# A hand-scheduled attention and routed-FFN kernel: GpSimd waits for VectorE behind each gather and scatter, and the schedule builder takes its settings from a table by chunk

## The chip, the cores and the metric

The kernel runs on one core of a Trainium2 chip. The metric is the device time of one launch in microseconds (us); lower is better. PE is TensorE, DVE is VectorE, ACT is ScalarE, POOL is GpSimd, and SP is the engine that issues most of the DMAs.

## What is computed

Eight batches, each with 3136 tokens of 256 features. First an attention without softmax, then a feed-forward step for the 128 best tokens of each batch:

```python
scores = (1 / S) * z @ z.T                     # z: 8 x 3136 x 64, symmetric scores
x = u * (np.maximum(scores, 0) ** 2 @ v)       # u, v: 8 x 3136 x 256
for b in range(8):
    s = x[b] @ w_gate
    top = the 128 tokens with the largest s
    h = np.maximum(x[b, top] @ w1, 0)          # w1: 256 x 1024
    out[b, top] = x[b, top] + sigmoid(s[top])[:, None] * (h @ w2)
```

## The kernel before

Each batch is cut into seven chunks of tokens (six of 512, one of 64), and each chunk into slots of pairs of key blocks. For a slot PE makes the scores (tile `sc`), ACT rectifies them into `a`, ACT or DVE squares `a`, and the square is split into two parts that PE can multiply at full rate: `hi` (a rounding, on ACT) and `lo` (the square less `hi`, a subtraction with two inputs in SBUF, on DVE or POOL). PE multiplies both parts with `V`, which is split in the same way, into the accumulator `acc`. The scores are symmetric, so DVE also transposes each square (`aT`), SP stores it to DRAM (`squares`), and later slots read it back (`qk`) in place of computing it; these are split too. At a chunk's end `acc` becomes `sum`, is multiplied with `u` (`ut`), transposed (`x`) and stored to `out`. PE works in halves of 64 rows, two at a time.

The routing of a batch runs beside the attention of the next ones. DVE counts against thresholds until the 128 tokens are found and forms their numbers (`ids`). POOL then gathers the rows from `out` with an indirect DMA (`xe<-out,ids`), PE runs the two layers, and POOL scatters the result back with another indirect DMA (`out<-y,ids`). There are 8 gathers, 8 scatters and one small first gather (`junk<-in_v`).

The order of all instructions on each engine is fixed when the kernel is built. A list scheduler keeps a model of the engines (class `Clock`) and a list of jobs for ACT, DVE, POOL and SP. `job` puts a job in, `begins_at` says when it could begin, `advance` emits the earliest one, and the loop at the end picks the next work for PE (`choices`, `emit`). Some constants set how eager it is: `NEAR` (how far ahead of PE the others are filled), `SPARE` (an extra cost of DVE when a `lo` may go to POOL or DVE), `EARLY` (how long an operand must have been ready before PE prefers it), `FAR` and a literal 2.0 (how long a step of the routing waits behind its operand), and `QUIET`. The model knows that an operation of POOL right behind an indirect DMA can hold up a DVE operation that is under way (`at_once` and `hold` in `note`). In the trace nearly every instruction carries the same helper's line (L265), so it is read by tile names.

Of the kernel before, what the change touches and what calls it, by code (L numbers as in the profile page):

```python
# [29 lines left out]
EARLY = 0.4  # L30
# [3 lines left out]
SPARE = 0.6  # L34
MARGIN = 0.3
QUIET = 9
SOON = -0.2
FAR = 4.0
SLACK = 2.0
WARM = 6.6  # L40
# [50 lines left out]
class Clock:  # L91
# [3 lines left out]
    def __init__(self):  # L95
        self.at = {"pe": 0.9, "act": 1.15, "dve": 0.85, "pool": 0.5, "sp": 0.75}
        self.queue = self.mark = 0.0
        self.writes, self.reads, self.before, self.rings = {}, {}, {}, {}
        self.port = {"dve": (0.0, 0.0), "pool": (0.0, 0.0)}
        self.newest, self.alone = {}, {"dve": 0.0, "pool": 0.0}  # L100
        self.kept = self.since = -1.0
        self.planned = self.known = False
        self.half, self.by_half, self.long = [0.0, 0.0], False, False
# [91 lines left out]
    def note(self, by, op, outs, ins):  # L195
# [171 lines left out]
def attention_then_routed_ffn(ctx: ExitStack, tc: tile.TileContext, zt, ut, v, wg, w1, w2, cst, cst16, keys, outs, at, cap):  # L367
# [87 lines left out]
    NEAR = 0.3  # L455
# [7 lines left out]

    def begins_at(j, e):
        if j.ok and not j.ok():
            return None
        rings = j.rings() if callable(j.rings) else j.rings
        if not all(x.free() for x in rings):
            return None
        ready = j.ready() if callable(j.ready) else j.ready  # L470
        ready = max([ready] + [x.when() + 0.05 for x in rings])
        t = max(clock.at[e], ready)
        if len(j.on) > 1:

            def done(o):
                t = max(clock.at[o], ready)
                a, z = clock.port.get({"pool": "dve", "dve": "pool"}.get(o), (0.0, 0.0)) if j.locks else (0.0, 0.0)
                return max(t + j.took[o], z + j.took[o] - 0.14 if a <= t < z else 0.0)

            if any(done(o) < done(e) for o in j.on if o != e):  # L480
                return None
        return t

    def advance(upto):

        while True:
            best = None
            for e, jobs in pending.items():
                if clock.at[e] >= upto + NEAR:
                    continue  # L490
                for j in jobs:
                    t = begins_at(j, e)
                    if t is None or t >= upto + NEAR:
# [12 lines left out]
    def quiet():  # L506

        k = now[0]
        if k >= kmax:
            return True  # L510
        b, c = slots[k][:2]
        n = len(todo.get(k, ()))
        return c == WHOLE or not (k == ends[b, c] and n <= QUIET or k == begins[b, c] and n >= 11 and c > 0)
# [63 lines left out]
    def takes(n):  # L577
        return {"pool": 0.15 + 0.00219 * n, "dve": 0.16 + 0.00104 * n + SPARE, "act": 0.19 + 0.00083 * n}

# [9 lines left out]
    def load_consts():  # L589
# [16 lines left out]
        nc.sync.dma_start(st[:, : cst16.shape[1]], cst16)  # L606
        zero_ids = moe.tile([P, 1], I32, name="zero_ids", tag="ids", bufs=3)
        nc.vector.memset(zero_ids, 0)
        job("pool", now[0], lambda e: first_gather(zero_ids), [zero_ids])
        job("pool", now[0] + 2, lambda e: use_consts(c_sb, st), lambda: max(clock.after(x) for x in (st, c_sb)) + SLACK)  # L610
        consts["run"] = w_run
# [13 lines left out]
    def more_consts():  # L625

        def place():
            consts["place"] = const.tile([P, 1], F32, name="place")
            nc.vector.tensor_reduce(consts["place"], consts["before"], axis=AX.X, op=ALU.add)
            consts["wg_col"] = const.tile([P, NK], F32, name="w_col")  # L630
            consts["wg_row"] = const.tile([P, NK, P], F32, name="w_row")

        def clear():
# [4 lines left out]
        def column(h):  # L638
            w_row, w_col = consts["wg_row"][:, h], consts["wg_col"][:, h : h + 1]
            nc.vector.scalar_tensor_tensor(  # L640
                w_row[:, :Q], consts["run"][:, h * Q : (h + 1) * Q], 1.0, consts["fold"][:, :Q],
                op0=ALU.mult, op1=ALU.mult, accum_out=w_col,
            )

        def row(h):
            nc.vector.tensor_scalar(consts["wg_row"][:, h], consts["ones"], consts["wg_col"][:, h : h + 1], None, op0=ALU.mult)

        ready = lambda: "ident" in consts and quiet()
        return [("dve", fn, (), (), ready) for fn in (place, clear, *[lambda f=f, h=h: f(h) for h in range(NK) for f in (column, row)])]
# [419 lines left out]
    def half_scores(k):  # L1069
# [27 lines left out]
        def high(e):  # L1097
            hi = hi_ring.take("hi", F32R)
            set_part(k, hi, None)
            for to in (hi[:REST, 0], hi[low_part, 1]):  # L1100
                nc.scalar.activation(to, st["a"], AF.Square, scale=1 / SCALE)
            took = {"dve": 0.16 + 0.00104 * CH + SPARE, "act": 0.3 + 0.00083 * CH}
            job("dve|act", k, square, [st["a"], st["s"], hi[:REST, 0], hi[low_part, 1]], took=took)
# [38 lines left out]
    def scores(k):  # L1142
# [22 lines left out]
        def rise(e):  # L1165
# [6 lines left out]
            else:  # L1172
                job("act", k, high, lambda: max(clock.after(st["a"]), room_when(k)) + 0.05, ok=lambda: room_for(k))
# [260 lines left out]
    def finish(b, c, h):  # L1434
# [10 lines left out]
        def total(e):  # L1445
# [4 lines left out]
            if merged(b) and c == FIFTH:  # L1450
                took["dve"] -= SPARE
# [510 lines left out]
    def route_both(couple, i):  # L1962
# [96 lines left out]
        def choose_both():  # L2059
# [9 lines left out]
            inside = st["ps"][:, 3 * P :]  # L2069
# [45 lines left out]
    def choose(st, r0):  # L2115
# [11 lines left out]
        inside = st["ps"][:, 3 * P :]  # L2127
# [219 lines left out]
    def scatter_of(couple, i):  # L2347
        b, st = couple["of"][i], couple["st"][i]
        nc.gpsimd.indirect_dma_start(outs[b], bass.IndirectOffsetOnAxis(ap=st["ids"], axis=0), couple["y"][:, i], None)

# [103 lines left out]
    def expert(b, st, n):  # L2454
# [21 lines left out]
        def gather():  # L2476
# [7 lines left out]
            )  # L2484
            st["xe"] = xe
# [176 lines left out]
        def scatter():  # L2662
            nc.gpsimd.indirect_dma_start(
                outs[b], bass.IndirectOffsetOnAxis(ap=st["ids"][:m, :], axis=0), st["y"][:m], None
            )

# [134 lines left out]
    at_slot(first_of[0, 3], lambda: chain_of(more_consts(), 5))  # L2801
# [43 lines left out]
    def step_when(x):  # L2845
# [6 lines left out]
        late = 0.1 if x.lag == 20 else 0.05 if x.lag in (-9, -20) else SOON if "gathered" in end else MARGIN if x.lag < 0 or closing else 2.0 if x.lag == 1 else FAR  # L2852
        return max([x.ready + late] + [clock.after(y) + late for y in reads] + [r.when() + 0.05 for r in rings])

    def choices():
# [12 lines left out]
        for n, (i, k, x) in enumerate(near_):  # L2868
# [6 lines left out]
            if t <= clock.at["pe"] + 0.02 - EARLY:  # L2875
                return got
# [62 lines left out]
    def begin_slot():  # L2939
        for fn in plan.pop(now[0], ()):  # L2940
# [11 lines left out]
    while now[0] < kmax or any(x.steps for x in chains) or any(pending.values()):  # L2952
# [4 lines left out]
        sure = [x for x in got if x[0] <= t + 0.02 - EARLY]  # L2957
# [47 lines left out]
```

## Time and profile before

| | |
|---|---|
| median of 3 runs | 2019.31 us (2017.54 to 2019.4) |
| the profiled execution's own time | 2021.63 us |
| its span, first to last instruction | 2019.9 us |
| PE busy | 1989.0 us, 98% of the span |
| DVE, ACT, POOL busy | 77%, 73%, 77% |
| mean granted clock of PE | 0.997 |

PE is busy nearly all the time. Busy time alone hides one thing: a matmul that runs at the lower of PE's two clock levels (1.2 instead of 2.4 GHz) is also busy, for longer.

### The profile page before, as it was taken

Reading aid. Unit: us, or ns where it says so; the run is one execution under the profiler, and the core shown is the slowest. Engines: PE = TensorE matmul, PEld = TensorE weight load, DVE = VectorE, ACT = ScalarE, POOL = GpSimd, SP = SyncE. Lnnn points to the kernel's source line nnn. Section 1 sums busy time; section 2 is a strip of 40 time slices with the busy share of each in tenths; the row PEclk is TensorE's granted clock in tenths of the full one; section 3 lists DMA queues with packets and bytes.
Section 4 is the critical chain, followed back from the end, with each engine's and each line's share of the span. In section 5 each row is a group of like instructions: output and inputs, shape, how many; then the busy total and the mean of one; then the engine's idle time right before and its main releaser. Section 6 shows DMA issues by size and latency. Waiting matters only on the chain. (4 is left out here: it accounts for less than half of the span.)

```text
span 2019.9 us, 45873 instructions
## 1 busy us (share of the span) xinstructions
PE 1989.0 (98%) x17311; PEld 1651.1 (82%) x17311; DVE 1553.6 (77%) x2585; ACT 1482.5 (73%) x1835; POOL 1558.8 (77%) x1095
## 2 busy tenths in 40 slices
PE   9999999999999999999999999999999999999998
PEld 6788878888788888788878889887788888878776
DVE  7776787667988767767798866797679676897886
ACT  8876688777877669776887657876578876877652
POOL 8798887779878677878888767796687777887762
PEclk9999999999999999999999999999999999999999
DMA  6989867876787867878767786777866868767862
GB/s 193 258 237 247 208 190 220 213 190 168 206 235 207 207 173 218 241 181 194 193 202 214 211 218 188 208 216 204 217 173 198 235 177 202 191 181 199 218 160 95
DMA packets 421615, 408.50 MB, mean 202 GB/s; under 512 B 128910, under 2 KB 329232, under 8 KB 421392
## 3 DMA queue, kind: packets, MB, share of 16 engines
q1 hardware_dynamic: 420224, 403.07, 74.3%
q8 instruction: 135, 2.21, 0.5%
q0 software_dynamic: 800, 2.10, 0.3%
q14 instruction: 88, 0.72, 0.1%
q10 hardware_dynamic: 368, 0.39, 0.1%
HBM read 230.08 MB, written 175.37 MB: 201 GB/s over the span
## 5 line engine op out<-in xcount | busy, mean ns | idle before, releaser
L265 PE MATMUL acc<-hi,V 64*128 64x512 f32 x8832 | 1176.7, 390 | 8.6 <-DVE sum L265 4.6
L265 PEld LDWEIGHTS acc<-hi,V 64*128 64x128 f32 x8832 | 865.9, 185 | 162.6 <-DVE sum L265 9.0
L265 PE MATMUL acc<-lo,V 64*128 64x512 f32 x4272 | 632.5, 390 | 2.5 <-POOL lo L265 1.6
L265 POOL TENSOR_TENSOR lo<-a,hi 128x512 fp32r<-128x512 f32 x308 | 467.6, 1528 | 175.4 <-ACT a L265 84.4
L265 POOL TENSOR_TENSOR lo<-qk,hi 128x512 fp32r<-128x512 f32 x313 | 481.5, 1553 | 83.5 <-ACT hi L265 58.6
L265 PEld LDWEIGHTS acc<-lo,V 64*128 64x128 f32 x4272 | 423.0, 185 | 82.8 <-POOL lo L265 8.5
L265 ACT ACTIVATE hi<-a 128x1024 fp32r<-128x1024 f32 (+2 forms) x390 | 353.6, 907 | 108.6 <-PE acc L265 85.6
L265 DVE STREAM_TRANSPOSE aT<-a 128x512 f32<-128x512 f32 (+2 forms) x622 | 383.5, 646 | 42.5 <-ACT a L265 30.4
L265 ACT ACTIVATE a<-a 128x1024 f32<-128x1024 f32 (+1 forms) x349 | 330.7, 949 | 79.1 <-DVE a L265 69.0
L265 DVE TENSOR_TENSOR lo<-a,hi 128x512 fp32r<-128x512 f32 x236 | 269.4, 1146 | 138.3 <-ACT a L265 61.1
L265 ACT ACTIVATE a<-sc 128x1024 f32<-128x1024 f32 (+2 forms) x344 | 324.8, 945 | 65.8 <-PE sc L265 35.7
L265 ACT CAST hi<-qk 128x1024 fp32r<-128x1024 f32 x240 | 249.8, 1047 | 127.7 <-PE acc L265 71.2
L265 DVE TENSOR_TENSOR lo<-qk,hi 128x512 fp32r<-128x512 f32 x167 | 176.5, 1068 | 51.4 <-ACT hi L265 45.1
L265 PE MATMUL sc<-ZH 64*128 64x512 f32 (+2 forms) x728 | 157.8, 380 | 5.8 <-DVE a L265 3.0
L265 PE MATMUL sc<-ZL,ZH 64*128 64x512 f32 (+2 forms) x728 | 156.4, 376 | 0.1
L265 POOL TENSOR_TENSOR lo<-own,hi 128x256 fp32r<-128x256 f32 x87 | 92.4, 1081 | 72.6 <-ACT hi L265 42.7
L265 POOL TENSOR_TENSOR ut<-x,w_run 128x512 f32<-128x512 f32 x90 | 135.8, 1520 | 11.8 <-DVE x L265 10.8
L265 PE MATMUL sc<-ZH,ZL 64*128 64x512 f32 (+2 forms) x680 | 136.3, 370 | 0.0
L265 PE MATMUL acc<-lent,V 64*128 64x512 f32 x1008 | 130.2, 390 | 2.9 <-DVE sum L265 1.4
L265 POOL TENSOR_TENSOR ut<-sum,ut 128x512 f32<-128x512 f32 x70 | 97.6, 1395 | 26.9 <-DVE sum L265 23.8
L265 PEld LDWEIGHTS acc<-lent,V 64*128 64x128 f32 x1008 | 97.7, 184 | 23.7 <-DVE sum L265 3.1
L265 DVE SCALAR_TENSOR_TENSOR a<-a 128x512 f32<-128x512 f32 (+2 forms) x85 | 100.2, 1186 | 19.5 <-ACT hi L265 13.1
(245 smaller groups left out, 1818.8 us busy)
## 6 DMA issues: line engine op xcount, KB each, us to landing
squares<-aT SPq DMA_DIRECT2D x240, 512.0 KB, 4.3
qk<-squares SPq DMA_DIRECT2D x480, 256.0 KB, 6.2
ut<-in_ut SPq DMA_DIRECT2D x48, 512.0 KB, 4.0
vst<-in_v SPq DMA_DIRECT2D x190, 128.0 KB, 3.1
out<-x SPq DMA_DIRECT2D x188, 128.0 KB, 4.1
squares_own<-aT SPq DMA_DIRECT2D x47, 256.0 KB, 2.0
own<-squares_own SPq DMA_DIRECT2D x188, 64.0 KB, 2.4
zst<-in_zt SPq DMA_DIRECT2D x85, 128.0 KB, 5.4
```

The lines of the kernel that those rows point to most:

```text
L265: got = None if self.clock.planned else real(*args, **kw)
```

## The change

Behind every gather and scatter of the main part, `breathe` adds three tiny operations. POOL clears a one-column tile `tick`; DVE clears it as well, which has to wait for POOL's; POOL clears it again, which has to wait for DVE's. While the DVE part is outstanding the scheduler emits nothing else on POOL, and it has the highest rank on DVE. The model takes 9 us in place of 3 for the landing of a gather.

The constants `NEAR`, `QUIET`, `SPARE`, `FAR`, `EARLY` and the literal 2.0 move into a dictionary, and a table `TASTE` replaces one of them from the start of 20 chunks on. Three smaller edits: the first gather moves from the load of the constants to a slot of the second chunk, the constants of the routing are weighed right behind their load, and in the first two slots `hi` gets a higher rank. A mask of the merge (`inside`) moves from PSUM to SBUF.

```diff
-EARLY = 0.4
-SPARE = 0.6
-QUIET = 9
-FAR = 4.0
+BASE = {"near": 0.3, "quiet": 9, "spare": 0.6, "mid": 2.0, "far": 4.0, "early": 0.4}
+TASTE = {(0, 1): {"early": 0.6}, (0, 5): {"early": 0.3}, (1, 0): {"far": 6.0}, ...
...
         elif op == "indirect_dma_start":
             self.at[by] = self.kept = self.since = begin + 1.0
-            end = max(begin + 3.0, self.queue + 2.0)
+            far = self.late and outs[0].space != bass.MemoryType.DRAM
+            end = max(begin + (9.0 if far else 3.0), self.queue + 2.0)
...
+    def breathe():
+
+        if now[0] >= kmax or "gathered" in end:
+            return
+        till = clock.since + 0.25
+        a = moe.tile([P, 1], F32, name="tick", tag="tick", bufs=1)
+        nc.gpsimd.memset(a, 0.0)
+        held_pool[0] = j = Job(["dve"], -1000, None, till, (), None, None, False)
+
+        def tick(e):
+            nc.vector.memset(a, 0.0)
+            nc.gpsimd.memset(a, 0.0)
+            held_pool[0] = None
+
+        j.fn = tick
+        pending["dve"].append(j)
+
     def begins_at(j, e):
-        if j.ok and not j.ok():
+        if e == "pool" and held_pool[0] is not None or j.ok and not j.ok():
             return None
...
-                job("act", k, high, lambda: max(clock.after(st["a"]), room_when(k)) + 0.05, ok=lambda: room_for(k))
+                soon = b == c == 0 and k < 2
+                job("act", k - 9 * soon, high, lambda: max(clock.after(st["a"]), room_when(k)) + 0.05 - 0.09 * soon * (k == 0), ok=lambda: room_for(k))
...
             nc.gpsimd.indirect_dma_start(
                 xe[:m], None, outs[b], bass.IndirectOffsetOnAxis(ap=ids[:m, :], axis=0)
             )
+            breathe()
...
     def begin_slot():
+        for key in TASTE:
+            if begins[key] == now[0]:
+                tune.update(BASE | TASTE[key])
+        clock.late = now[0] < kmax
```

The built programs show what moves. PE multiplies the same amount in both: 14,112 products `acc<-hi`, `acc<-lo` and `acc<-lent` together, and as many scores. `tick` stands 26 times on POOL and 13 times on DVE. The order changes on all engines and over the whole program, since every choice follows from the ones before.

The first place is POOL at the gather of batch 4 (`out_4`); the numbers tell buffers apart. Before:

```order
L265 TENSOR_TENSOR lo_19492<-qk_18915,hi_19467 128x512
L265 DMA xe_19529<-out_4,ids_19512 128x256
L265 TENSOR_TENSOR lo_19542<-a_19479,hi_19519 128x512
L265 TENSOR_TENSOR lo_19564<-qk_19160,hi_19559 128x512 x2
L265 TENSOR_TENSOR lo_19647<-own_19433,hi_19638 128x256 x2
```

And POOL at the same gather in the changed program:

```order
L265 TENSOR_TENSOR lo_19708<-qk_19191,hi_19706 128x512
L265 DMA xe_19724<-out_4,ids_19699 128x256
L265 MEMSET tick_19726 128x1 x2
L265 TENSOR_TENSOR lo_19765<-a_19718,hi_19742 128x512
L265 TENSOR_TENSOR lo_19783<-qk_19373,hi_19770 128x512 x2
```

Three subtractions stood straight behind the gather; now the two clearings stand between, the second of which waits for DVE.

The second place is DVE around the same gather, from the making of `ids` on. Before:

```order
L265 TENSOR_TENSOR ids_19512<-ids_19508,at_19513 128x1
L265 TENSOR_REDUCE gate_18518<-ut_18997 128x16
L265 TENSOR_TENSOR lo_19542<-a_19479,hi_19519 128x512
L265 STREAM_TRANSPOSE aT_19568<-a_19479 128x4x128
L265 TENSOR_TENSOR a_19566<-sc_19561,a_19566 64x512 x2
```

And DVE there in the changed program:

```order
L265 TENSOR_TENSOR ids_19699<-ids_19691,at_19700 128x1
L265 TENSOR_TENSOR lo_19708<-qk_19191,hi_19706 128x512
L265 MEMSET tick_19726 128x1
L265 TENSOR_TENSOR lo_19765<-a_19718,hi_19742 128x512
L265 STREAM_TRANSPOSE aT_19791<-a_19718 128x4x128 x2
```

The subtraction `lo<-a` that DVE shares with POOL (one half each) now stands behind the tick on both engines; other work has moved as well.

The third place is ACT at the start of the program, from the cast of the second piece of `ZH` on. Before:

```order
L265 CAST ZH<-zall 128x4x4x32
L265 ACTIVATE a<-sc 128x1024 x3
L265 ACTIVATE hi<-a 128x1024
L265 CAST ZH<-zall 128x4x4x32
L265 ACTIVATE a<-a 128x1024
```

And in the changed program:

```order
L265 CAST ZH<-zall 128x4x4x32
L265 ACTIVATE a<-sc 128x1024
L265 ACTIVATE hi<-a 128x1024
L265 ACTIVATE a<-sc 128x1024 x2
L265 ACTIVATE hi<-a 128x1024
```

The first `hi` stands behind one rectification instead of three.

## Rows read from the trace of the kernel before

**Rows 1.** Windows: time, busy us and instructions of PE, PEld, DVE, ACT, POOL; clock.

```profile
core 0: us, PE busy (x) PEld busy (x) DVE busy (x) ACT busy (x) POOL busy (x), PEclk, DMA share, GB/s
60.00:1370.00 1310.00, 1302.62 (x11527) 1092.90 (x11525) 1010.78 (x1602) 991.64 (x1217) 1040.69 (x723) 1.00 0.78 209
1370.00:1400.00 30.00, 27.38 (x227) 23.39 (x225) 20.35 (x28) 17.88 (x24) 18.39 (x16) 0.94 0.87 217
...
1450.00:1480.00 30.00, 27.21 (x211) 20.96 (x209) 19.51 (x17) 14.07 (x23) 23.75 (x19) 0.89 0.80 193
1480.00:1990.00 510.00, 505.64 (x4381) 416.17 (x4378) 412.43 (x807) 370.20 (x459) 389.45 (x275) 1.00 0.71 192
```

**Rows 2.** Timeline of PE, 1376 to 1392 us: start, length, instructions, idle before.

```profile
1380.33 2.02 PE L265 MATMUL acc<-hi,V 64*128 64x512 f32 x16
1382.18 1.08 PE L265 MATMUL acc<-lo,V 64*128 64x512 f32 x8
1385.88 0.39 PE L265 MATMUL sc<-ZH 64*128 64x256 f32 x2 [2.62 <-DVE a L265]
...
1386.31 3.52 PE L265 MATMUL acc<-hi,V 64*128 64x512 f32 x16
```

**Rows 3.** Timeline of DVE, 1376 to 1392 us.

```profile
1379.22 4.59 DVE L265 TENSOR_TENSOR lo<-a,hi 128x512 fp32r<-128x512 f32 x1
...
1384.37 1.36 DVE L265 TENSOR_TENSOR a<-sc,a 64x512 f32<-64x512 f32 x2
```

**Rows 4.** Timeline of POOL, 1376 to 1392 us.

```profile
1378.46 1.01 POOL L265 DMA_INDIRECT xe<-out,ids  x1 [1.29 <-DVE ids L265]
1379.48 1.29 POOL L265 TENSOR_TENSOR lo<-a,hi 128x512 fp32r<-128x512 f32 x1
1380.74 2.53 POOL L265 TENSOR_TENSOR lo<-qk,hi 128x512 fp32r<-128x512 f32 x2
```

**Rows 5.** The page's groups: count, busy us, mean ns of one, idle before.

```profile
L265 DVE TENSOR_TENSOR lo<-a,hi 128x512 fp32r<-128x512 f32 x236 | 269.4, 1146 | 138.3 <-ACT a L265 61.1 <-issue 37.7 <-POOL lo L265 28.9
```

**Rows 6.** Timeline of DVE, 1451 to 1478 us.

```profile
1453.82 8.45 DVE L265 TENSOR_TENSOR hi<-a,hi 64x512 fp32r<-64x512 f32 x1
```

**Rows 7.** Timeline of POOL, 1451 to 1478 us.

```profile
1453.14 1.01 POOL L265 DMA_INDIRECT out<-y,ids  x1 [0.16 <-issue]
1454.18 1.31 POOL L265 TENSOR_TENSOR ut<-x,w_run 128x512 f32<-128x512 f32 x1
1455.45 5.02 POOL L265 TENSOR_TENSOR lo<-qk,hi 128x512 fp32r<-128x512 f32 x4
1460.44 1.28 POOL L265 TENSOR_TENSOR ut<-x,w_run 128x512 f32<-128x512 f32 x1
```

**Rows 8.** Timeline of PE, 1451 to 1478 us.

```profile
1462.33 0.73 PE L265 MATMUL acc<-hi,V 64*128 64x512 f32 x3 [0.84 <-DVE hi L265]
...
1464.34 3.22 PE L265 MATMUL acc<-hi,V 64*128 64x512 f32 x16 [1.28 <-ACT hi L265]
1468.18 2.07 PE L265 MATMUL acc<-lo,V 64*128 64x512 f32 x8 [0.62 <-POOL lo L265]
...
1470.05 1.91 PE L265 MATMUL acc<-hi,V 64*128 64x512 f32 x6
```

**Rows 9.** Timeline of ACT, 0 to 24 us.

```profile
6.98 1.93 ACT L265 ACTIVATE a<-sc 128x1024 f32<-128x1024 f32 x2
...
10.18 1.05 ACT L265 ACTIVATE hi<-a 128x1024 fp32r<-128x1024 f32 x1
```

**Rows 10.** Timeline of POOL, 0 to 24 us.

```profile
8.79 1.38 POOL L265 TENSOR_TENSOR V<-vst,V 128x512 fp32r<-128x512 f32 x1 [0.37 <-DMA vst<-in_v]
```

**Rows 11.** Timeline of PE, 0 to 62 us.

```profile
11.28 0.49 PE L265 MATMUL acc<-hi,V 64*128 64x512 f32 x1
...
14.85 0.50 PE L265 MATMUL acc<-lo,V 64*128 64x512 f32 x2 [0.65 <-DVE lo L265]
```

**Rows 12.** Groups of all instructions: small operations of DVE and POOL.

```profile
L265 DVE TENSOR_SCALAR own_rest<-c_sb 128x128 fp32r<-128x128 f32 x1 | 1.3, 1252 | 0.0
...
L265 DVE MEMSET zero_ids<- 128x1 int32 x1 | 0.1, 59 | 0.0
```

**Rows 13.** Groups of POOL: the shortest clearing.

```profile
L2994 POOL MEMSET const-float32-0.0<- 128x1 f32 x1 | 0.1, 98 | 0.2 <-issue 0.2
```

More of the change, by code (lines that the diff above doesn't have):

```diff
@@ L102, in __init__ @@
         self.planned = self.known = False
+        self.late = True
         self.half, self.by_half, self.long = [0.0, 0.0], False, False
@@ L488, in advance @@
             for e, jobs in pending.items():
-                if clock.at[e] >= upto + NEAR:
+                if clock.at[e] >= upto + tune["near"]:
                     continue
@@ L492, in advance @@
                     t = begins_at(j, e)
-                    if t is None or t >= upto + NEAR:
+                    if t is None or t >= upto + tune["near"]:
                         continue
@@ L512, in quiet @@
         n = len(todo.get(k, ()))
-        return c == WHOLE or not (k == ends[b, c] and n <= QUIET or k == begins[b, c] and n >= 11 and c > 0)
+        return c == WHOLE or not (k == ends[b, c] and n <= tune["quiet"] or k == begins[b, c] and n >= 11 and c > 0)
     def calm():
@@ L606, in load_consts, with first_ids @@
         nc.sync.dma_start(st[:, : cst16.shape[1]], cst16)
+        job("pool", now[0] + 2, lambda e: use_consts(c_sb, st), lambda: max(clock.after(x) for x in (st, c_sb)) + SLACK)
+        for h in range(NK):
+            job("dve", now[0] + 4, lambda e, h=h: weigh_consts(h, w_run), ok=lambda: "ident" in consts)
+    def first_ids():
         zero_ids = moe.tile([P, 1], I32, name="zero_ids", tag="ids", bufs=3)
@@ L636, in clear @@
             consts["own_rest"] = own_rest
[L638 to L649, printed above, removed]
+        w_row, w_col = consts["wg_row"][:, h], consts["wg_col"][:, h : h + 1]
+        nc.vector.scalar_tensor_tensor(
+            w_row[:, :Q], w_run[:, h * Q : (h + 1) * Q], 1.0, consts["fold"][:, :Q], op0=ALU.mult, op1=ALU.mult, accum_out=w_col
+        )
+        nc.vector.tensor_scalar(w_row, consts["ones"], w_col, None, op0=ALU.mult)
     W = 2 * F
@@ L1450, in total @@
             if merged(b) and c == FIFTH:
-                took["dve"] -= SPARE
+                took["dve"] -= tune["spare"]
             job("pool|dve", k, weigh, here, ok=lambda: (b, c) in chunk, took=took)
@@ L2068, in choose_both @@
             nc.vector.tensor_scalar(what[:, :P], st["ps"][:, :P], ends[:, 2:], None, op0=ALU.add)
-            inside = st["ps"][:, 3 * P :]
+            inside = moe.tile([P, P], F32, name="inside", tag="hh", bufs=2)
             rank = consts["rank"][:, :P]
@@ L2126, in choose @@
         begin = st["begin"]
-        inside = st["ps"][:, 3 * P :]
+        inside = moe.tile([P, P], F32, name="inside", tag="hh", bufs=2)
         rank = consts["rank"][:, r0 : r0 + P]
@@ L2484, in gather @@
             )
+            breathe()
             st["xe"] = xe
@@ L2665, in scatter @@
             )
+            breathe()
         def first_weights(e):
@@ L2800, in attention_then_routed_ffn @@
     at_slot(SLOTS + 4, lambda: chain_of(steps, 5))
-    at_slot(first_of[0, 3], lambda: chain_of(more_consts(), 5))
+    at_slot(first_of[0, 1] + 8, lambda: job("dve", now[0] + 1, lambda e: first_ids()))
     issued = 0
@@ L2851, in step_when @@
         closing = now[0] > ends[B - 1, FIFTH] - CLOSE
-        late = 0.1 if x.lag == 20 else 0.05 if x.lag in (-9, -20) else SOON if "gathered" in end else MARGIN if x.lag < 0 or closing else 2.0 if x.lag == 1 else FAR
+        late = 0.1 if x.lag == 20 else 0.05 if x.lag in (-9, -20) else SOON if "gathered" in end else MARGIN if x.lag < 0 or closing else tune["mid"] if x.lag == 1 else tune["far"]
         return max([x.ready + late] + [clock.after(y) + late for y in reads] + [r.when() + 0.05 for r in rings])
@@ L2874, in choices @@
                 continue
-            if t <= clock.at["pe"] + 0.02 - EARLY:
+            if t <= clock.at["pe"] + 0.02 - tune["early"]:
                 return got
@@ L2956, in attention_then_routed_ffn @@
         got = choices()
-        sure = [x for x in got if x[0] <= t + 0.02 - EARLY]
+        sure = [x for x in got if x[0] <= t + 0.02 - tune["early"]]
         soon = sure or [x for x in got if x[0] <= t + 0.02]
```

20 lines of the change are left out of this document (10 added, 10 removed).

## The prediction, before the changed kernel ran

> **What bounds the kernel now.** I first read busy time by engine, then cut the span into stretches and looked for those in which PE does fewer matmuls than elsewhere, and there read PE, DVE and POOL side by side. In the 1310 us from 60 on, PE is idle for 1310 - 1302.6 = 7.4 us and starts a matmul every 1310 / 11527 = 0.1136 us; in the 510 us from 1480 on it is idle for 4.4 us [rows 1]. So PE is the bound, its work is the same before and after, and a change can only give back idle time and slow time. Two short stretches stand out: 227 and 211 matmuls in 30 us each, at granted clocks of 0.94 and 0.89, where 0.1136 us each would have let them end in 25.8 and 24.0 us. That is 4.2 + 6.0 = 10.2 us lost in 60 us, nearly as much as all other idle time between 60 and 1990 us (7.4 + 4.4 = 11.8).
>
> Both have one cause. In the first, POOL issues a gather for 1.01 us and starts three subtractions straight behind it, the last of which ends at 1380.74 + 2.53 = 1383.27 [rows 4]. A DVE subtraction that began at 1379.22, while the gather was being issued, takes 4.59 us and ends at 1383.81 [rows 3]; its kind has a mean of 1146 ns [rows 5]. So it ends 0.54 us behind POOL's last, and is some 3.4 us late. Behind it on DVE stand the two halves of `a<-sc` (1384.37, the sum of a score tile from PE), and PE's next score waits for them: 2.62 us idle, and the 16 products behind that take 3.52 us where 16 took 2.02 us just before [rows 2], that is at the 1.2 GHz level for most of it. Sum 2.62 + 1.50 = 4.1 us.
>
> In the second, a scatter is followed by six POOL operations without a pause, until 1460.44 + 1.28 = 1461.72 [rows 7]; a DVE operation that began at 1453.82, again inside the issue, takes 8.45 us and ends at 1462.27, 0.55 us behind POOL's last [rows 6]. PE then idles 0.84 + 1.28 + 0.62 = 2.74 us and runs 16 products in 3.22, 8 in 2.07 and then six in 1.91 us, where 16 took 2.02 and 8 took 1.08 us [rows 2, 8]: 1.20 + 0.99 + 0.83 = 3.0 us more. Sum 5.8 us. The two ways of counting agree: 9.9 by pieces, 10.2 by numbers of matmuls.
>
> **The wait behind each gather and scatter.** It puts POOL to rest behind the indirect DMA until DVE has passed the tick. A DVE operation caught in the issue can then end, as both caught ones did some 0.5 us after POOL paused, and no chain of POOL operations follows before it has. I take the whole 10.0 us back. Bounds: nothing (rivals below), and 10.2 plus what the lateness did further on, say 11.
>
> Its cost: 13 clearings on DVE, of which a like one takes 59 ns, and 26 on POOL at about 98 ns [rows 12, 13]: 0.8 and 2.5 us in 2020, on engines that are busy for three quarters of the time. More weighty is the meeting itself. DVE takes its queue in order; if it reaches the tick as POOL begins the issue it stands for 1.01 + 0.10 = 1.1 us, and behind it stand transposes and the `lo` and `hi` parts for PE. Or POOL stands for one DVE operation (1.1 us), with its own `lo` parts behind. In the first bad stretch a DVE delay of 3.4 us cost PE 4.1 us, so 1.1 us costs at most 1.3, or 17 us for 13 meetings if each hit PE in full; at least nothing, since parts are made up to three slots ahead. The nearest row to it is the idle time of PE between 60 and 1990 us outside the two stretches, 11.8 us in all [rows 1], although DVE waited 28.9 us for POOL's parts in front of this one kind of subtraction alone [rows 5]: of a microsecond by which DVE stands, little reaches PE. I take +0.8, a twentieth of the upper bound.
>
> **First high parts sooner.** The first `hi` ran from 10.18 to 11.23 behind three rectifications; behind one it can start near 6.98 + 0.97 = 7.95 (half of the two that take 1.93) and end near 9.0 [rows 9]. PE's first product came at 11.28 [rows 11]. It also needs the low part of `V`, ready at 8.79 + 1.38 = 10.17 [rows 10], so it comes 1.1 us sooner, not 2.2. Next PE needs `lo`, which came at 14.85 after a hole of 0.65 us [rows 11], and `lo` needs DVE to square `a` first. So between 0 and 2.2 us; I take -1.0.
>
> **Constants and first gather.** The DVE work on constants moves ahead; the one piece with a row of any size takes 1252 ns [rows 12]. All of it is done in one burst now, in the crowded first 100 us. If all of that piece hit PE it would cost 1.3 us, if none, nothing; +0.5. The first gather moves to a later place with a tick behind it, and the mask in SBUF replaces an operation of equal size: no term of their own.
>
> **The table.** It moves the order of everything, PE's work kept. What it can win is the 11.8 us of holes; what it can lose has no such ceiling, but the old order was made by the same rules with one value throughout, so holes of the same kind and total are the natural guess. Bounds -7 and +7; I take -2.0, since the longer modelled landing also keeps DVE and PE from standing behind gathered rows that have not come.
>
> **Sum** against the profiled execution: 2021.63 - 10.0 + 0.8 - 1.0 + 0.5 - 2.0 = 2009.9 us. The median of the runs shown lies 2.3 us under that execution, so 2009.9 - 2.3 = 2007.6; I say 2007.5.
>
> **A rule that speaks against it.** In the rows, the caught DVE operations wait for three and for six POOL operations that started after them [rows 3, 4, 6, 7]. The Trainium skill, page "SBUF — State Buffer", section "Who interferes with whom", says that the port pair which the two engines share is a lock: whichever starts first has it for its whole instruction. By that a DVE operation waits for at most the one POOL operation under way, and the trace does not agree: 4.59 and 8.45 us. Were the rule the whole story, the change would take away little, which is the third rival.
>
> **Rivals.** (1) The table and the start give more than I grant: the holes of 11.8 us halve and the start gives 2: 1997 to 2002. For it: most holes are single events under 1 us; against: the settings differ little. (2) The new order makes new holes, 4 to 8 us more than the old: 2011.5 to 2016. For it: no order of this length is free of surprises, the old one had two large ones. (3) POOL's chain is not what holds DVE, and the wait frees it of only one POOL operation, 1.29 us of the 3.4 us in the first stretch [rows 4] and as much of about 7.5 in the second: 1.29 / 3.4 x 4.1 + 1.29 / 7.5 x 5.8 = 2.6 us in place of 10.0, so 2007.5 + 7.4 = 2015. Against it: both ends follow POOL's last operation by 0.54 and 0.55 us. (4) The change doesn't do what it says: DVE's operation stays held while POOL rests, because it waits for the transfer and not for POOL; then POOL stands as well, and the time is 2018 to 2022. Against it the same two ends. (5) The other side: the tick is first in DVE's line and DVE reaches it before POOL has begun to issue, at most of the 13 places. Full price 1.3 us each, 17 us, in place of my 0.8 gives 2023.7, slower. It decides from about 1.25 us at each place; for it, POOL is the later engine at many gathers, as it waits for `ids` [rows 4]; against it, POOL's waiting is for DVE, which then has just made them.
>
> **Chances.** Likeliest 0.60, with a range of its own of 2002 to 2012; (1) 0.14; (2) 0.13; (3) 0.05; (4) 0.04; (5) 0.04. Faster by over 0.2% (4 us, about what a measurement can tell), that is under 2015.3: the likeliest, (1), most of (2) and half of (3), 0.87. Within: 0.08. Slower: 0.05. The range for 8 in 10 leaves out the ends of (1) and all of (3) to (5): 1999 to 2015.
>
> **What would show it.** Right: no DVE operation over 2.5 us behind a gather or scatter; `tick` on POOL with idle time of about 1 us before its second; no stretch between 60 and 1990 us with a granted clock under 0.97; holes of PE there of 6 to 14 us. The start: the first product near 10.2 us. Wrong: a long DVE operation that ends although POOL rests (4), PE waits whose releaser is DVE right behind a tick (5), or new holes of 2 us and more with a drop of the clock far from any gather (2).

## The result and the profile after

The changed kernel is slower: 2032.56 us median of 6 runs (2029.95 to 2037.48) against 2020.14 us of 6 runs of before; ratio 1.0064, 95% interval 1.0046 to 1.0082. I had said 2007.5, with 2015 as the upper end.

The work of the wait can be seen. Timelines of POOL and of DVE at the scatter that in before was followed by the stall of 8.45 us [rows 6, 7]:

```profile
1463.31 1.02 POOL L265 DMA_INDIRECT out<-y,ids  x1 [1.23 <-DVE y L265]
1464.33 0.12 POOL L265 MEMSET tick<- 128x1 f32 x1
1465.18 0.10 POOL L265 MEMSET tick<- 128x1 f32 x1 [0.73 <-DVE tick L265]
1465.24 2.24 POOL L265 TENSOR_TENSOR lo<-qk,hi 128x512 fp32r<-128x512 f32 x1
```

```profile
1463.68 0.68 DVE L265 TENSOR_TENSOR hi<-a,hi 64x512 fp32r<-64x512 f32 x1
1464.40 0.70 DVE L265 STREAM_TRANSPOSE aT<-a 64x512 f32<-64x512 f32 x1
```

The same subtraction `hi<-a` begins within the issue again and takes 0.68 us; that this is the wait's doing is a question for experiments 2 and 8. No DVE operation of this execution takes more than 2.31 us. What the meetings cost the two engines (groups: count, busy us, mean ns | idle before):

```profile
L265 DVE MEMSET tick<- 128x1 f32 x13 | 0.8, 59 | 7.2 <-POOL tick L265 7.2
L265 POOL MEMSET tick<- 128x1 f32 x26 | 2.8, 108 | 4.6 <-DVE tick L265 4.4 <-ACT a L265 0.2
```

Busy 0.8 and 2.8 us as forecast, and 7.2 and 4.4 us of standing. But PE has other losses now. Windows, columns as in [rows 1]:

```profile
60.00:1180.00 1120.00, 1109.29 (x9768) 928.97 (x9766) 862.91 (x1335) 845.72 (x1030) 887.19 (x629) 1.00 0.79 207
1180.00:1200.00 20.00, 18.15 (x146) 14.05 (x146) 13.89 (x23) 13.41 (x20) 12.85 (x12) 0.91 0.79 212
1200.00:1325.00 125.00, 122.95 (x1112) 102.81 (x1109) 96.87 (x144) 90.17 (x117) 71.94 (x54) 1.00 0.68 190
1325.00:1345.00 20.00, 17.40 (x138) 14.37 (x138) 13.93 (x38) 13.35 (x16) 14.86 (x12) 0.91 0.92 228
1345.00:1990.00 645.00, 638.86 (x5533) 527.39 (x5531) 493.83 (x951) 464.31 (x575) 499.06 (x365) 1.00 0.77 202
```

The two slow stretches of before are gone (clock 1.00 from 1345 on). Two others are there, at a clock of 0.91, and a third lies near the end (0.83 from 1985 to 1995 us). PE is idle for 23.4 us between 60 and 1990 (the lengths less the busy times: 10.7 + 1.9 + 2.1 + 2.6 + 6.1), where in before it was 11.8 outside its two slow stretches and 5.4 in them [rows 1]. What stands ahead of the two new ones, timelines of ACT, POOL, DVE and PE:

```profile
1189.49 0.62 ACT L265 CAST ZH<-zst 128x512 fp32r<-128x512 f32 x1 [2.97 <-DMA zst<-in_zt]
```

```profile
1330.00 1.70 POOL L265 TENSOR_TENSOR ut<-sum,ut 128x512 f32<-128x512 f32 x1 [2.69 <-DMA ut<-in_ut]
```

```profile
1329.89 0.69 DVE L265 TENSOR_TENSOR ut<-sum,ut 128x512 f32<-128x512 f32 x1 [1.74 <-DMA ut<-in_ut]
```

```profile
1191.11 1.19 PE L265 MATMUL acc<-hi,V 64*128 64x512 f32 x8 [0.67 <-ACT hi L265]
1192.74 0.50 PE L265 MATMUL acc<-lo,V 64*128 64x512 f32 x2 [0.44 <-POOL lo L265]
1193.98 0.65 PE L265 MATMUL acc<-lo,V 64*128 64x512 f32 x2 [0.73 <-POOL lo L265]
...
1332.98 0.74 PE L265 MATMUL acc<-lo,V 64*128 64x512 f32 x4 [2.60 <-POOL lo L265]
```

Each time an engine that takes its queue in order has come to a small operation on loaded data, the load hasn't landed, and the `hi` or `lo` that PE needs stands behind it.

To compare kernels whose orders differ I lined up their traces by the matmul work that PE had done (each matmul counted by its columns) and compared, for each stretch of about 20 us of work, the time that passed. Where the stretches are cut moves a single figure by up to about 1 us. The differences to the profiled execution of before, in us, at the places where any is large (named by the time in before; "start" is 31 to 117 us):

| kernel | start | 654 | 817 | 1191 | 1272 | 1314 | 1336 | 1402 | 1446 | 1473 | 1993 | rest | all |
|---|---|---|---|---|---|---|---|---|---|---|---|---|---|
| after | +0.5 | +2.4 | +2.0 | +3.9 | +1.6 | +0.1 | +3.3 | -3.7 | +0.2 | -6.3 | +3.1 | +1.7 | +8.8 |
| all 13 meetings alone (1) | +1.1 | 0 | +0.1 | 0 | 0 | 0 | 0 | -3.6 | +0.1 | -2.4 | 0 | +0.7 | -4.1 |
| after without meetings (2) | +0.4 | +2.5 | +2.5 | +3.5 | +2.0 | +0.1 | +2.7 | -3.7 | +0.2 | -6.3 | +1.2 | +3.2 | +8.3 |
| after, mask in PSUM (3) | +0.1 | -0.3 | +2.5 | +6.0 | +4.4 | +0.1 | +2.3 | -3.7 | +0.2 | -6.0 | +3.1 | +2.7 | +11.3 |
| after, empty table (4) | +0.2 | +2.4 | -0.3 | +0.4 | +0.1 | +0.1 | +1.4 | -3.5 | -0.3 | -3.4 | 0 | +7.3 | +4.2 |
| table alone (6) | 0 | -0.2 | +2.4 | +5.7 | +1.1 | 0 | +1.2 | -4.5 | +0.1 | -0.6 | +1.1 | +3.9 | +10.1 |
| table but two, alone (9) | -0.2 | -0.3 | +3.0 | +0.1 | +1.6 | +4.1 | +0.1 | -4.0 | +5.5 | -6.8 | +1.1 | +5.6 | +9.7 |
| loads not waited for (13) | +0.2 | +2.5 | +1.8 | -0.2 | +2.3 | +0.1 | -0.9 | -3.7 | +2.3 | -4.5 | +2.9 | +5.6 | +8.3 |

The two stalls gave back 10.0 us (1402 and 1473), and all else together took 18.8. One execution of each kernel is shown here (the spans of these two differ by 8.4 us), and that of before lay 1.5 us above its median, so the sums are told by the medians below.

### The profile page after: what moved, and what is told of

It is laid out like the page before. It is cut to its first block, busy times and chain, and to the rows that moved or that the text cites. A ratio compares the mean times of both kernels' runs of the same rounds, so it can differ in the third digit from the quotient of the medians.

```text
span 2028.3 us, 45885 instructions
## 1 busy us (share of the span) xinstructions
PE 1990.9 (98%) x17303; PEld 1651.6 (81%) x17303; DVE 1548.8 (76%) x2605; ACT 1486.0 (73%) x1838; POOL 1540.1 (76%) x1111
## 4 chain that ended last, share of the span: by engine, by line
PE 66%; DMA 11%; DVE 7%; ACT 5%; issue 5%; POOL 3%; SPq 2%; POOLq 0%; ACTq 0%; DVEq 0%
PE acc L265 56%; PE sc L265 8%; DMA qk<-squares 3%; POOL lo L265 2%; ACT a L265 2%; SPq L265 2%; ACT hi L265 2%; DMA vst<-in_v 1%; DVE lo L265 1%; DVE aT L265 1%; DMA ut<-in_ut 1%; DMA squares<-aT 1%; DVE a L265 1%; DMA rest<-squares_last 1%; DMA squares_own<-aT 1%
## 5 line engine op out<-in xcount | busy, mean ns | idle before, releaser
L265 DVE TENSOR_TENSOR lo<-a,hi 128x512 fp32r<-128x512 f32 x241 | 260.8, 1088 | 135.7 <-ACT a L265 79.4
L265 DVE TENSOR_TENSOR lo<-qk,hi 128x512 fp32r<-128x512 f32 x168 | 166.9, 1007 | 49.1 <-ACT hi L265 42.1
L265 POOL TENSOR_TENSOR lo<-own,hi 128x256 fp32r<-128x256 f32 x93 | 97.5, 1068 | 73.3 <-ACT hi L265 48.1
L265 PE MATMUL acc<-lent,V 64*128 64x512 f32 x912 | 114.7, 389 | 2.0 <-DVE sum L265 1.3
L265 POOL TENSOR_TENSOR ut<-sum,ut 128x512 f32<-128x512 f32 x63 | 86.4, 1374 | 32.2 <-DVE sum L265 25.4
L265 POOL TENSOR_TENSOR V<-vst,V 128x512 fp32r<-128x512 f32 (+1 forms) x67 | 93.0, 1399 | 13.5 <-ACT V L265 13.2
```

What stands on the lines that cost most here:

```text
L265: got = None if self.clock.planned else real(*args, **kw)
```

## The experiments

The ratios are to runs of before on the same chip, with their 95% intervals; the medians of before were 2019.9, 2019.8, 2020.0 and 2022.0 us for experiments 1 to 4, 5 to 8, 9 to 12 and 13 to 15.

**1. All 13 meetings, in the order of before.** The planner doesn't see them:

```
+        known(lambda: (nc.gpsimd.memset(a, 0.0), nc.vector.memset(a, 0.0), nc.gpsimd.memset(a, 0.0)))
```

> The order of before on every engine, with nothing added but the 13 meetings: behind each gather and scatter a clearing of a small tile on GpSimd, one of it on VectorE, and another on GpSimd. Theory A (the wait is worth what was forecast, and the loss of the changed kernel comes from its new order): both stalls of before go, 10.0 us, and 13 meetings cost 0.8: 9 us faster than before, near 2011; no VectorE operation above 2.5 us behind a gather. Theory B (the meetings themselves cost the 22 us by which the changed kernel missed): the stalls go but the meetings cost as much or more: the same as before or up to 12 us slower. Theory C (the stall is only moved, VectorE stays held at the tick): the same as before, 2018 to 2022, with the long VectorE operations still there.

2018.14 us, ratio 0.9994 (0.9985 to 1.0003): 1.8 us less by the medians, inside the interval, and not 9. Theory B has this time, but not for this reason: away from the two stalls the lined-up trace loses only 2.0 us. The held operations are gone, the first stall is given back (3.6), but of the second only 2.4 us. The windows, and timelines of PE, ACT and POOL there:

```profile
1450.00:1480.00 30.00, 26.84 (x233) 20.98 (x231) 14.36 (x18) 15.45 (x24) 27.54 (x22) 1.00 0.83 193
```

```profile
1459.92 0.63 PE L265 MATMUL acc<-hi,V 64*128 64x512 f32 x4
...
1461.83 2.12 PE L265 MATMUL acc<-hi,V 64*128 64x512 f32 x16 [1.14 <-ACT hi L265]
1465.55 1.20 PE L265 MATMUL acc<-lo,V 64*128 64x512 f32 x8 [1.60 <-POOL lo L265]
```

```profile
1460.64 0.63 ACT L265 ACTIVATE hi<-a 128x512 fp32r<-128x512 f32 x1 [6.44 <-issue]
```

```profile
1452.55 1.78 POOL L265 TENSOR_TENSOR ut<-x,w_run 128x512 f32<-128x512 f32 x1
1454.28 5.01 POOL L265 TENSOR_TENSOR lo<-qk,hi 128x512 fp32r<-128x512 f32 x4
1459.24 1.31 POOL L265 TENSOR_TENSOR ut<-x,w_run 128x512 f32<-128x512 f32 x1
1461.86 1.83 POOL L265 TENSOR_TENSOR lo<-own,hi 128x256 fp32r<-128x256 f32 x2 [1.31 <-ACT hi L265]
```

The held subtraction `hi<-a` now begins at 1452.47 us, behind the tick and 0.27 us after the end of the issue, and takes 0.69 us. PE's two waits behind ACT's `hi` and POOL's `lo` (1.28 and 0.62 us in before [rows 8]) are there as 1.14 and 1.60 us, without any held operation. Only the third wait and the slow clock (0.89 in before, 1.00 now) were the stall's. POOL has done the same six operations by 1460.55 and then stands for 1.31 us, as ACT's `hi` isn't there; and ACT, after 6.44 us of idle time, starts that `hi` at 1460.64, 0.09 us behind the end of the products that PE began at 1459.92. In before it starts 0.09 us behind PE's products too (1463.15, the products of 1462.33 + 0.73 us). So it seems to wait for a `hi` buffer that these products free; no run varied the number of buffers. At the first gather the meeting makes a new wait: the tick is next in DVE's queue, and `a<-a`, behind it, starts after 2.61 us of idle time, when POOL has issued. Timeline of DVE:

```profile
52.33 1.22 DVE L265 SCALAR_TENSOR_TENSOR a<-a 128x1024 f32<-128x1024 f32 x1 [2.61 <-ACT V L265]
52.35 0.06 DVE L265 MEMSET tick<- 128x1 f32 x1
```

**2. The changed order without its meetings.** They are planned and not issued.

> The order of the changed kernel on every engine, with the three clearings of each meeting left out, so that GpSimd doesn't wait. Theory A (the meetings cost next to nothing and guard against stalls): as slow as the changed kernel or slower, by 4 to 6 us for each VectorE operation that gets caught in the issue of a gather; 2033 to 2045. Theory B (the meetings are the loss): 10 to 20 us faster than the changed kernel, 2013 to 2023.

2036.75 us, ratio 1.0088 (1.0072 to 1.0104): as slow as with them, or some us slower, theory A. The meetings are not the loss. But in this order they hardly guard anything: timelines of POOL and DVE at the place of the second stall,

```profile
1463.60 1.02 POOL L265 DMA_INDIRECT out<-y,ids  x1 [1.22 <-DVE y L265]
1465.19 1.28 POOL L265 TENSOR_TENSOR lo<-qk,hi 128x512 fp32r<-128x512 f32 x1 [0.57 <-ACT hi L265]
```

```profile
1463.97 0.68 DVE L265 TENSOR_TENSOR hi<-a,hi 64x512 fp32r<-64x512 f32 x1
```

The operation begins within the issue, and isn't held: POOL happens to stand for 0.57 us behind it (though 8 shows one that isn't held without such a pause). One subtraction of the whole run is held, to 2.28 us. So the changed order has the 6.3 us at 1473 without the wait too.

**3. The mask in PSUM again**, the changed order kept: `inside` is `st["ps"][:, 3 * P :]`, and the planner counts it as in SBUF.

> The order of the changed kernel on every engine, with one difference: the mask is written in PSUM again, as before. Theory M (the mask in SBUF takes a place at the memory that GpSimd holds: its operations take 1.26 to 1.35 us in place of 0.35): they go back to 0.35 us, and the 1.29 and 0.82 us holes of PE behind the first of them, near 640 us, and some of those near 1165 and 1842 go: 2 to 4 us faster than the changed kernel. Theory N (those operations are long for another reason, or nothing waits for them): within 1 us of it.

2033.7 us, ratio 1.0062 (1.0043 to 1.0081): no difference that can be measured in the total (theory N by that), since this kernel's other losses vary from run to run (2025.28 to 2038.07). At its place theory M is plain. Timelines of DVE in the changed kernel and in this one:

```profile
633.90 1.35 DVE L265 TENSOR_SCALAR inside<-c_sb,ends 128x128 f32<-128x128 f32 x1
635.28 2.58 DVE L265 SCALAR_TENSOR_TENSOR oh<-c_sb,ends,inside 64x128 bf16<-64x128 f32 x2
```

```profile
635.85 0.73 DVE L265 SCALAR_TENSOR_TENSOR oh<-c_sb,ends,upto 64x128 bf16<-64x128 f32 x2
```

The holes of PE behind the first pair (1.29 us, then 0.82) are gone, 2.7 us at 654.

**4. An empty table.** `TASTE = {}`

> The changed kernel with an empty table: the base settings hold throughout, and the order is planned anew. Theory T (the table's settings are what makes the new holes): they go, and with the stalls given back the time is 2010 to 2018. Theory O (any new order of this program draws its own holes, whatever the settings, since its planner doesn't know how late transfers land): another total of holes, as far from that of the changed kernel as that of before, in either direction: 2015 to 2040, with the holes at other places, behind VectorE, ScalarE or GpSimd operations that wait for a transfer.

2026.96 us, ratio 1.0035 (1.0021 to 1.0048): the table costs about 6 us. The losses at 817, 1191, 1272 and 1993 go, as in theory T; smaller ones come elsewhere, as in theory O, and the time is in O's range and not in T's.

**5. Twelve meetings, in the order of before.** As 1, without the call behind the first gather.

> The order of before on every engine and 12 of the 13 meetings: the one behind the first gather, at 51 us, is left out. In the profile of the run with all 13, VectorE stands 2.61 us in front of that meeting and the stretch from 31 to 97 us loses 1.5 us more than before. Theory F (a meeting costs where VectorE reaches it before GpSimd has issued, and this is the one such place): those 1.5 us come back, so 1 to 1.5 us under the run with all 13 and 2.5 to 4 us under before, 2016 to 2017.5. Theory G (without the meeting the hold of 3.3 us at 52 us comes back and costs as much): the same time as with all 13.

2016.83 us, ratio 0.9984 (0.9975 to 0.9993), 3.0 us less than before (1.4 to 5 by the interval). The time is that of theory F, but the interval overlaps that of 1. At the place itself F holds, with 0.8 us: with the meeting PE waits for 0.40 us at 54.75, where it otherwise has no wait, and for 1.16 us at 60.56, where it otherwise waits for 0.74. The hold at 52 us is back (two subtractions in 3.90 us) and costs PE less than the meeting did. This is the lowest median of the study, under both kernels; the intervals of 1, 11 and 12 overlap its own.

**6. The table alone**, in before.

> Before with the table by chunk and nothing else of the change: no meetings, the old landing model, the old start, the mask in PSUM. The order is planned anew. Theory T (the table is a bad one, whatever stands around it): 4 to 8 us slower than before, 2024 to 2028, as the changed kernel is 6 us slower than the same with an empty table. Theory O (the table's loss in the changed kernel is a chance meeting of its order with late transfers): some other difference, between 5 us faster and 10 us slower, with holes at other places than in the changed kernel.

2028.04 us, ratio 1.0039 (1.0026 to 1.0053): 8 us slower, with losses at two of the same places, 817 and 1191. Theory T.

**7. The changed kernel with an empty table, the mask in PSUM and the constants spread as before.**

> The changed kernel with three parts undone: the table empty, the mask in PSUM and the constants spread as before. What is left of the change: the meetings with their planning, the landing of 9 us in the model, the late first gather and the early first high parts. Theory P (the parts add up by their holes: the mask 2.4 us and the constants 1.3 us in the profile of the run with an empty table): 3.7 us under that run, so 2023. Theory O (undoing them gives a third order with its own holes): not 2023 but anywhere between 2015 and 2035, the holes near 80 and 640 us gone and others come.

2022.0 us, ratio 1.0013 (1.0004 to 1.0022), 5 us under 4. Theory P by the time; 654 and the start are as in before or better. Theory O's range holds it too, and some losses did move (2 us near 1535 us that 4 doesn't have).

**8. A change without meaning.**

```
-            end = begin + took + 0.175
+            end = begin + took + 0.17
```

> Before with one number of the planner's model of TensorE changed, the constant behind the end of a matmul from 0.175 to 0.170 us, which has no meaning for the chip. The order changes at some places (the instructions are the same). Theory O (new orders differ by several us through chance meetings): 2 us or more away from before in either direction. Theory S (only meaningful changes of the order cost): within 1 us of before, 2019 to 2021.

2018.4 us, ratio 0.9998 (0.9989 to 1.0007): the same. Theory S, for this one reshuffle. In the traced execution the second hold doesn't occur, which gives 2.9 us at 1473, as in 1. POOL and DVE have the order of before there. Timelines of POOL and DVE:

```profile
1453.63 1.01 POOL L265 DMA_INDIRECT out<-y,ids  x1 [0.16 <-issue]
1454.66 1.50 POOL L265 TENSOR_TENSOR ut<-x,w_run 128x512 f32<-128x512 f32 x1
1456.12 5.04 POOL L265 TENSOR_TENSOR lo<-qk,hi 128x512 fp32r<-128x512 f32 x4
```

```profile
1454.30 0.69 DVE L265 TENSOR_TENSOR hi<-a,hi 64x512 fp32r<-64x512 f32 x1
```

The subtraction begins 0.67 us into the issue (0.68 in before [rows 6, 7]), the same POOL operations follow without a pause, and it takes 0.69 us in place of 8.45. So being caught in the issue does not always mean being held.

**9 and 10. Two of the table's entries emptied**, in 6 and in the changed kernel: `(3, 1): {}, (3, 5): {}`

> Before with the table alone, as in the run with the table alone, but with two of its 20 entries emptied: the one for sequence 3 from chunk 1 (near 0.8) and the one from its chunk 5 (far 6.0, in force until chunk 5 of sequence 4). In the run with the table alone the two largest new losses, 4.1 us near 817 us and 5.7 us near 1191 us, lie in the stretches in which these two are in force. Theory E (those two entries make those two losses): both go, 2018 to 2021, that is 8 to 10 us under the table alone. Theory O (the order after any change of the table meets other late transfers): the losses move elsewhere, 2023 to 2032.

> The changed kernel, everything in it but the same two entries of the table. Theory E: its 2.8 us near 817 and 3.9 us near 1191 us go (there they are, at the same places), 2025 to 2028. Theory O: as slow as the changed kernel, 2030 to 2038, with losses at other places.

2029.45 us, ratio 1.0038 (1.0025 to 1.0051), and 2033.15 us, ratio 1.0062 (1.0048 to 1.0076). Theory E falls: 1191 is gone in both, 817 isn't, and as much is lost at other places (1314 and 1446 in the first): theory O. In 9 PE itself waits for a weight:

```profile
1447.65 0.73 PE L263 MATMUL y<-wh,hh 128*128 128x256 f32 x4 [0.34 <-DMA wh<-w2h_there]
1450.69 1.22 PE L263 MATMUL y<-wl,hh 128*128 128x256 f32 x4 [2.31 <-DMA wl<-w2l_there]
```

**11. Number 7 with the old landing**, `begin + 3.0` in place of 9.0.

> The lean version (empty table, mask in PSUM, constants spread), with the planner's landing of a gather at 3 us as before in place of 9. Theory L (the long landing pushes work behind the gathers aside and makes what the lean version still loses against the old order with 12 meetings, 5 us): 2017 to 2019. Theory K (the 9 us are right, gathered rows land that late, and with 3 TensorE stands behind them): 2024 or more, with holes of TensorE behind the gathered rows. Theory N (no part of it): within 2 us of the lean version.

2018.39 us, ratio 0.9992 (0.9984 to 1.0001), 3.6 us under 7. Theory L, in this order.

**12. Number 5 with the first high parts in front.**

> Before with 12 meetings (none behind the first gather) and the first high parts in front of the third rectification, nothing else. The order differs from before only near the start. Theory H (the first high parts give 1.0 us, as forecast): 1 us under the run with 12 meetings, 2015 to 2016.5, the first product near 10.2 us. Theory J (the start is bound by something else, so nothing, or the planner pays it back later): 2016.5 to 2020.

2018.6 us, ratio 0.9992 (0.9983 to 1.0001), 1.8 us over 5, with intervals that overlap: theory J, in which nothing is gained. Against 5 it gains 2.5 us near 55 us and loses 1.2 near 31, 0.5 near 76, 1.0 near 97 and 1.5 near 303. Its traced execution ran at the lower clock level from 10.8 to 14.2 us (14 products in 3.36 us), which those of 5 and of the changed kernel did not, and so says little of the start.

**13. Three waits for loads taken out of the changed kernel**, its order kept.

```
+        other = src if (b, i) != (5, 4) else consts["all"][:, :CH]
...
+            known(nc.vector.transpose, rest_u, consts["wg"][:REST, : 2 * P] if b == 2 else st["u"])
```

> The changed kernel, its order the same on every engine, with three waits for loads taken away by other data: the part of u that VectorE turns at 807 us and the part of z that ScalarE rounds at 1189 us (and GpSimd subtracts from) are read from a constant tile, and the load of u awaited at 1330 us is left out, its product taken with a constant tile. So the values of those parts are not those of the reference. Theory W (the changed order loses because it puts one engine in line behind a load that lands late): the losses near 817, 1191 and 1336 us, 2.8 + 3.9 + 3.3 us over before, go at those places, and the time is 8 to 10 us under the changed kernel, 2023 to 2026. Theory V (the order is too crowded at those places, the late load is only what is seen last): at most 3 us in all, 2030 to 2034.

2027.91 us, ratio 1.0030 (1.0017 to 1.0043), where the changed kernel had 1.0064: some 6.5 us back, between the two theories. The losses at 1191 and 1336 are gone (-0.2 and -0.9). Theory W at two of the three places. Timelines of ACT and POOL: without the wait,

```profile
1187.91 0.62 ACT L265 CAST ZH<-c_sb 128x512 fp32r<-128x512 f32 x1
```

```profile
1325.99 1.29 POOL L265 TENSOR_TENSOR ut<-sum,c_sb 128x512 f32<-128x512 f32 x1
```

and the timeline shows no hole of PE from 1175 to 1200 and from 1320 to 1345. At 817 the loss stayed; there DVE came sooner to the next two transfers and stood:

```profile
808.93 0.71 DVE L265 STREAM_TRANSPOSE aT<-a 128x512 f32<-128x512 f32 x1 [2.56 <-DMA squares<-aT]
...
814.37 1.30 DVE L265 STREAM_TRANSPOSE x<-ut 128x512 f32<-128x512 f32 x2 [2.19 <-DMA out<-xr]
```

**14 and 15. The old start in 11, and the old landing in the changed kernel.**

> The lean version with the old landing of 3 us, and the first high parts at their old place as well; the order differs from that version near the start. Theory J (the first high parts cost 1.8 us, as they did beside the 12 meetings): 1.5 to 2 us under it, 2016.5. Theory H (they give 1.0 us, and what was measured beside the 12 meetings was another loss further on): 1 us over it, 2019.5.

> The changed kernel with the planner's landing of a gather at 3 us as before, everything else in it. Theory L (the long landing costs what it costs in the lean version, 3.6 us): 2029 to 2030. Theory O (beside the table it meets other late loads, and its price there is another): the same as the changed kernel or slower, 2032 to 2040.

2020.44 us, ratio 0.9996 (0.9987 to 1.0004), against 0.9992 for 11: theory H if any, but within the intervals. And 2045.19 us, ratio 1.0115 (1.0101 to 1.0130), beyond both theories: with 3 us the changed kernel is some 10 us slower by the ratios, and with 9 us the lean one 4 us slower. Theory L falls as a rule; the price of the model hangs on the rest of the order.

The trace of 15 has a hold of its own. Timelines of DVE, POOL and PE:

```profile
1342.31 7.45 DVE L265 TENSOR_TENSOR ZL<-zst,ZH 128x512 fp32r<-128x512 f32 x1
```

```profile
1342.90 3.82 POOL L265 TENSOR_TENSOR lo<-a,hi 128x512 fp32r<-128x512 f32 x3
1346.66 2.55 POOL L265 TENSOR_TENSOR lo<-qk,hi 128x512 fp32r<-128x512 f32 x2
```

```profile
1351.98 0.20 PE L265 MATMUL tot<-cnt,c 64*128 64x15 bf16 x2 [3.32 <-DVE cnt L265]
```

It ends at 1349.76, 0.55 us behind POOL's last, like the two of before, and PE stands for 3.32 us; but the nearest gather or scatter lies 40 us back. All 13 meetings are in this kernel, and none of them could guard it.

## Why the prediction was wrong

**"I take the whole 10.0 us back."** Right for the first stall of the traced execution (3.6 of 4.1). For the second the step failed that added all of PE's idle time and slow time behind the held operation: of 5.8 us the wait gives 2.4 in the old order (1). (The 5.8 is 6.0, since its last term sets six products against the time of eight; six take 0.84 elsewhere in this trace, at 55.74 us.) I had not asked what is late next: ACT's `hi` is as late as before, and POOL's next `lo` behind it.

A second step failed that I didn't see as one: I took what one execution lost for what every execution loses. The mean granted clock is on record for 85 later runs of before on four chips. 10 of them have 0.997, as the profiled execution had with its low stretches of 3.4 us (from 1386.5) and 6.8 us (from 1465.0); 27 have 0.998, 32 have 0.999, and 16 have 1.000. The means of these groups are 2023.0, 2021.2, 2019.8 and 2018.8 us: 4.2 us from the first to the last. So most runs of before lack at least one of the two slow stretches, and by this reading the sum counted a part twice: 10.0 us for the stalls, and then another 2.3 us because the median of the runs lies under that execution. (None of the 85 was traced; that a higher clock there means a missing stall is read from the clock alone. That a hold can stay out shows in 8, and that a hold of 8.44 us can leave the clock at 1.00 in the trace of 6, from 1464.06.) By the medians the meetings are worth 3.0 us at best (5). That the sum at 1402 and 1473 in the changed kernel is 10.0, as forecast, is a coincidence: it has most of it without any meeting (2).

The cause that I gave, being caught in the issue, doesn't fit all runs either: 8 has an operation caught and not held, 15 one held far from any issue. And in 1 the wait doesn't free a caught operation, as I had it: behind the tick no operation of DVE is caught, as it can start only when the issue is over.

**Cost of the meetings, +0.8.** Right in size: 12 of them can't be told from nothing, and the thirteenth, at the first gather, costs PE 0.8 us at its place, as DVE reaches it ahead of POOL and stands for 2.61 us, the mechanism of rival (5) at one place. The changed kernel moves that gather to 87 us, where it costs nothing seen.

**The start, -1.0.** The first product came at 9.54 us, 1.7 us sooner (I said 1.1). Timeline of PE:

```profile
9.54 0.49 PE L265 MATMUL acc<-hi,V 64*128 64x512 f32 x1
```

The low part of `V` held up only the products behind it: the bulk of them starts at 10.61, where before it was 11.39, and the first `lo` product at 14.15, where before it was 14.85. What is left of these 0.7 us further on is +1.8 in one order (12) and -0.8 in another (14), both within the intervals. This stays open.

**Constants, +0.5, and the mask, no term.** The burst stands where I put it, but is longer, as four `w_row` operations take 1.24 to 1.30 us each and PE stands for 0.95 us behind it (timelines of DVE and PE):

```profile
71.37 1.30 DVE L265 SCALAR_TENSOR_TENSOR w_row<-w_run,c_sb 128x32 f32<-128x32 f32 x1
...
72.72 1.24 DVE L265 TENSOR_SCALAR w_row<-c_sb,w_col 128x128 f32<-128x128 f32 x1
```

```profile
78.86 0.50 PE L265 MATMUL sc<-ZH 64*128 64x512 f32 x1 [0.95 <-ACT a L265]
```

1.4 us at that place. "An operation of equal size" was wrong for the mask: of the same size, but in another memory, the first of its operations at 633.90 took 1.35 in place of 0.35 us, and the two behind it 1.28 and 1.27. Undoing both gave 5 us (7 against 4), where I had 0.5; 2.4 of it lay at 654 and about 1 near the start, the rest came with the new order.

**The table, -2.0.** Wrong in sign: +6 beside the change (4), +8 alone (6). The step that failed is "holes of the same kind and total are the natural guess". What the runs showed in its place, at 1191 and 1336: a setting that moves operations by a few us moves them ahead of loads that have not landed, and the planner's clock doesn't know that they land late (13). "The longer modelled landing also keeps DVE and PE from standing" is not shown either way: it cost 4 us in one order (11) and saved some 10 in another (15).

So rival (2) came true, new holes, to which I gave 0.13 and 4 to 8 us. In the traced executions the stalls gave back 10.0 us and all else took 18.8, so it was undersized more than twofold. One way back, by medians against their own before: +12.4 us for the changed kernel, +7.1 without the table (4), +2.2 with mask and constants undone too (7), -1.6 with the old landing as well (11). Since each step plans a new order, these are not the prices of the parts in any other one. Of the mechanism, shown are the two waits for loads in 13 and the mask in 3; that all other new losses have the same cause is argued from their releasers only.

## What to carry to other kernels

A stall on an engine off the bound is worth what the bounding engine gets back when it is gone, so look for the next late operand before adding up all idle time behind it. A profile is one execution: see in several runs whether a stall is there each time before it goes into a sum. Where a scheduler writes the order, every changed setting is a new kernel: try each part by itself on the order that is known good, as the meetings were here, for 3 us gained in place of 12 lost. An operation moved to another memory is a new operation, with a price to look up.

## What the runs showed of the hardware

- In all traces of this study, each subtraction of DVE with two inputs in SBUF that took 1.9 us or more (0.68 us where nothing holds one) ended 0.54 to 0.56 us behind the end of an unbroken row of POOL operations: a row of three for 4.59 us, of six for 8.45 us. A pause of 0.07 us ended one of 2.28 us (2, at 797.55, in the midst of two POOL operations), a pause of 0.30 us that at 52.46 in before. Most began within an indirect issue, but not that of 7.45 us in 15 or shorter ones of 1.95 to 2.11 us in 7, 12 and 14; and in 8 one that began within it was not held. What decides is not known.
- The same DVE operations on the mask (128x128 and 64x128) took 0.28 to 0.35 us each at some places of the changed kernel and 0.95 to 1.44 us at others, with the mask in SBUF, and 0.34 to 0.36 us everywhere with it in PSUM (3).
- A hole of 1.14 and one of 1.60 us, 2.1 us apart, left the granted clock at 1.00 (1); holes of 0.67, 0.44 and 0.73 us within 3.6 us were in a stretch with 0.91 in the changed kernel.
- In the changed kernel the load of 512 KB awaited at 1330 us was issued at 1319.86 (SP's timeline): 10 us, in a stretch with a DMA share of 0.92; the median of its 48 like loads is 8.2 us.
